# Sixteen pairs of heads transposed by transfers inside SBUF, their tokens loaded 96 apart

## The chip, the cores and the metric

The kernel runs on one core of a Trainium2 chip. The core has five engines that run side by side: TensorE (PE, matmuls and transposes), VectorE (DVE), ScalarE (ACT), GpSimd (POOL) and SyncE (SP, which here only issues transfers), and 16 DMA engines that carry them out. The metric is the time of one execution on the device in microseconds (us), lower is better. Three runs of the kernel before took 293.79, 295.81 and 297.07 us; their median is 295.81 us.

## The reference

An attention layer with a few "beacon" keys in front, then a feed-forward layer whose three inner products go through a maximum:

```
B, H, S, Nb, D = 8, 8, 576, 16, 64
k_all, v_all = concat(beacon_k, k), concat(beacon_v, v)      # 592 keys
scores = q @ k_all.T / sqrt(D)        # causal on the 576, beacons always seen
attn   = softmax(scores) @ v_all
x = attn as (4608 tokens, 512)
h = max(x @ w1, x @ w2, x @ w3)       # 512 -> 768
out = h @ w_out                       # 768 -> 512, fp32
```

## The kernel before

**Units.** Two heads of one batch are a pair; there are 4 pairs per batch and 32 in all (p = 4 * batch + place). For the scores a pair needs q and k with the 64 features of both heads on the 128 partitions and the tokens along the free dimension. This transposed form lies in the tile `qkT`, which has `NT` = 4 slots (pair p uses slot p % 4), each with a q part and a k part of 16 beacon columns and 576 tokens.

**Three ways into `qkT`.** The first four pairs have a way of their own. Twenty of the other pairs (4 to 15, and the even ones from 16 on) go by `load_cast`: POOL issues two transfers that read fp32 from DRAM and write bf16 to a tile `p16`; one burst before the pair is needed, `turn_cast` makes 24 transposes on PE into PSUM, and two copies (the q part by ACT, the k part by DVE) bring them to `qkT`. The eight odd pairs from 17 on (the list `BY_DMA`) go by transfers: `load_pair` has SP load q and k as fp32 into a tile `st`, `cast_pair` casts them to bf16 on POOL, `store_pair` writes that to a scratch tensor `qk_dram` in DRAM, and `fetch_pair` brings it back with one transposing transfer. In both ways partition j of the loaded tile holds the six consecutive tokens 6j to 6j+5 of a head, which is one run of 1536 bytes in DRAM.

**The loop.** From batch 1 on, the causal part of the scores of a batch is cut into 13 windows of 512 columns, and three windows make a burst; there are 31 bursts, c = 0 to 30, and a pair's scores take a little over one. `loop` writes the order of the work out by hand, burst by burst, each engine and queue in that order: the score matmuls of the burst's windows (`emit_window`, with the exponential on ACT), two units of the feed-forward layer, the beacon columns and the PE transposes of pairs that the next burst needs, the masks on POOL, the products with v for pairs whose scores were done in the burst before (`emit_pv`), the stores of finished output rows, what stands in `late` (`store_pair` four bursts and `fetch_pair` two bursts ahead of the pair's first burst), then the casts on POOL that are due (`jobs`), and feed-forward units up to a fixed count of about 5.08 per burst. A block of 512 tokens is 18 units of the first product and 4 of the second, so about one block per batch.

**Loads.** `jobs` also sets the loads: the loads for SP (v in two pieces per batch, and the pairs of `BY_DMA`) stand in one list; four are issued at the start, and each cast then issues the next one. A load lands in one of 5 `st` buffers, so that it waits for the cast five loads before it.

**The attention output.** From batch 2 on, when the last pair of a batch is through, SP issues five transposing transfers (`fetch_x`, one per 128 tokens, from the tile `x` in SBUF to `xT` in SBUF) in that burst, behind the loads of the same burst. A feed-forward block waits for those of them that hold its tokens.

**SP's order.** Everything that SP issues (output rows, loads, stores to scratch, fetches of pairs and of x) leaves in program order; an entry that waits holds back those behind it.

The lines that the texts below name: 146 `load_pair`, 182 `cast_pair`, 194 `load_cast`, 220 `load_v`, 278 `store_pair`, 284 `fetch_pair`, 326 and 332 `turn_cast` (transposes, copies), 414 scores, 443 masks, 467 products with v, 505 `fetch_x`, 530 and 544 first product, 560 second product, 591 output stores.

Of the kernel before, what the change touches and what calls it, by code (L numbers as in the profile page):

```python
# [9 lines left out]
BF16 = mybir.dt.bfloat16  # L10
# [6 lines left out]
def kernel(  # L17
# [13 lines left out]
    nc = tc.nc  # L31

    B, H, S, D = q.shape
    Nb = beacon_k.shape[2]
    NK = S + Nb
# [7 lines left out]
    PPB = H // 2  # L43
    NPAIR = B * PPB
# [13 lines left out]
    QR = 6  # L58
    QP = S // QR
# [3 lines left out]
    part_p = [(hi - lo) // HR for lo, hi in part_tok]  # L63


    BY_DMA = [p for p in range(4 * PPB, NPAIR) if p % 2]
    X_PE = [0, 1]

    const = ctx.enter_context(tc.tile_pool(name="const", bufs=1))
# [1 line left out]
    pair_pool = ctx.enter_context(tc.tile_pool(name="pair", bufs=6))  # L71
# [2 lines left out]
    ffn_h = ctx.enter_context(tc.tile_pool(name="ffn_h", bufs=2))  # L74
    ffn_y = ctx.enter_context(tc.tile_pool(name="ffn_y", bufs=6))
    psum = ctx.enter_context(tc.tile_pool(name="psum", bufs=1, space=PSUM))
    dram_pool = ctx.enter_context(
        tc.tile_pool(name="dram", bufs=len(BY_DMA), space=bass.MemoryType.DRAM)
    )

    w_in = [const.tile([128, n_ct, d_ff], BF16, name=f"w{i}_sb") for i in range(3)]
    w_out_sb = const.tile([128, n_ft, d_model], BF16, name="w_out_sb")
# [18 lines left out]
    ident = const.tile([128, 128], BF16, name="ident")  # L101
# [3 lines left out]
    NT = 4  # L105
    qkT = const.tile([128, NT, 2, NKP], BF16, name="qkT")
# [31 lines left out]
    def load_pair(p, gate=None):  # L138
        b, pi = divmod(p, PPB)
        hs = slice(2 * pi, 2 * pi + 2)  # L140
        st = new_stage(("pair", p))
        if gate:
            gate.memset(st[0:QP, 0:1], 0.0)
            gate.memset(st[0:QP, NQ2 : NQ2 + 1], 0.0)
        for i, src in enumerate((q, k)):
            nc.sync.dma_start(
                out=st[0:QP, i * NQ2 : (i + 1) * NQ2].rearrange("p (h x) -> p h x", h=2),
                in_=src[b, hs].rearrange("h (p r) d -> p h (r d)", r=QR),
            )

    def part_source(i, h0, n, part):
# [26 lines left out]

    def cast_pair(p, cast):
        st = stage.pop(("pair", p))  # L180
        t16 = pair_pool.tile([QP, QR, 4, D], BF16, name="p16")
        cast(
            t16.rearrange("p r x d -> p x r d"),
            st[0:QP].rearrange("p (x r d) -> p x r d", x=4, r=QR),
        )
        stage["pair16", p] = t16

    def load_cast(p):
        b, pi = divmod(p, PPB)
        hs = slice(2 * pi, 2 * pi + 2)  # L190
        t16 = pair_pool.tile([QP, QR, 4, D], BF16, name="p16")
        t16 = t16.rearrange("p r x d -> p (r x d)").rearrange("p (x r d) -> p x r d", x=4, r=QR)
        for i, src in enumerate((q, k)):
            nc.gpsimd.dma_start(  # L194
                out=t16[:, 2 * i : 2 * i + 2].rearrange("p h r d -> p h (r d)"),
                in_=src[b, hs].rearrange("h (p r) d -> p h (r d)", r=QR),
            )
        stage["cast", p] = t16
# [72 lines left out]

    qk_dram = {}

    def store_pair(p):
        qk_dram[p] = dram_pool.tile([S, 4 * D], BF16, name="qk_dram")
        nc.sync.dma_start(
            out=qk_dram[p].rearrange("(p r) x -> p (r x)", r=QR),
            in_=stage.pop(("pair16", p)).rearrange("p r x d -> p (r x d)"),  # L280
        )

    def fetch_pair(p):
        nc.sync.dma_start_transpose(out=qkT[:, p % NT, :, Nb:NK], in_=qk_dram.pop(p))

    def turn_part(p, part, q_copy, k_copy):
        lo, hi = part_tok[part]
        n = part_p[part]
        for i in range(2):
            src = stage.pop(("part16", p, part, i))  # L290
            pb = one_bank().bitcast(BF16)[:, 0 : hi - lo]
            for r in range(HR):
                for e in range(2):
                    nc.tensor.transpose(
                        pb[64 * e : 64 * e + 64, r * n : (r + 1) * n],
                        src[:, e, r],
                        ident[0:n, 0:n],
                        tile_position=(0, 64 * e),
                    )
            dst = qkT[:, p % NT, i, Nb + lo : Nb + hi]  # L300
            (q_copy, k_copy)[i](
                dst.rearrange("d (p r) -> d p r", r=HR), pb.rearrange("d (r p) -> d p r", r=HR)
            )

    def turn_pair(p, q_copy, k_copy):
        src = stage.pop(("pair16", p))
        for i in (1, 0):
            pb = one_bank().bitcast(BF16)[:, 0:S]
            for r in range(QR):
                nc.tensor.transpose(  # L310
                    pb[:, r * QP : (r + 1) * QP],
                    src[:, r, 2 * i : 2 * i + 2].rearrange("p h d -> p (h d)"),
                    ident[0:QP, 0:QP],
                )
            (q_copy, k_copy)[i](
                qkT[:, p % NT, i, Nb:NK].rearrange("d (p r) -> d p r", r=QR),
                pb.rearrange("d (r p) -> d p r", r=QR),
            )

    def turn_cast(p, q_copy, k_copy):  # L320
# [310 lines left out]
    def L(fn, *a):  # L631
        return lambda: fn(*a)
# [167 lines left out]
    for b in range(2, B):  # L800
        c = first_burst[PPB * b]
# [18 lines left out]
    def X(b):  # L820
        avail[0] = S * (b + 1)
# [3 lines left out]
    def loop():  # L825
        nb = len(bursts)
        turns_x = []
        late = {}
        for p in range(PPB + 1, NPAIR):
            c = first_burst[p]  # L830
            if p in BY_DMA:
                late.setdefault(c - 4, []).append(L(store_pair, p))
                late.setdefault(c - 2, []).append(L(fetch_pair, p))
        for c, burst in enumerate(bursts):
            for w in burst:
                if w != ahead:
# [114 lines left out]
```

## Time and profile before

| | |
|---|---|
| profiled execution, own time | 294.89 us |
| its span on the core | 293.2 us |
| granted PE clock, mean | 0.994 |
| median of three runs without profile | 295.81 us |
| PE busy | 280.0 us, 95% of the span |
| DVE, ACT, POOL busy | 203.0, 123.5, 125.6 us |
| DMA moved | 43.37 MB in 89174 packets |

The span runs from the first to the last instruction of the program; the profiled execution's own time is 1.7 us longer. Busy time says how much an engine did, and the chain that ended last says what the end waited for. A transfer has two durations: how long the issuing queue was held (the duration of the issue), and how long until the data had landed. DMA packets are the pieces into which a transfer is cut; most of this kernel's are 256 bytes.

### The profile page before, as it was taken

The numbers are of one execution on the slowest core, as the hardware profiler recorded it, in microseconds if no ns is written. First come the engines' busy times: TensorE is split into PE (matmuls) and PEld (weight loads), VectorE is DVE, ScalarE is ACT, GpSimd is POOL, SyncE is SP. The second block draws the span as 40 slices with busy tenths as digits, with TensorE's granted clock in tenths as the row PEclk, the third lists the DMA queues.
The fourth block names the chain that finished last, engine by engine and source line by source line (L and its number), as shares of the span: only waits on it lengthen the run. The fifth ranks groups of instructions, "written<-read, shape, count | busy, mean of one in ns | idle before, by whom it ended". The sixth has DMA issues, their size and how long they took to land.

```text
span 293.2 us, 8074 instructions
## 1 busy us (share of the span) xinstructions
PE 280.0 (95%) x3146; PEld 161.4 (55%) x3146; DVE 203.0 (69%) x408; ACT 123.5 (42%) x270; POOL 125.6 (43%) x256
## 2 busy tenths in 40 slices
PE   7798897799999999999999999999999999999995
PEld 4566674366555555545555688755545554444442
DVE  4675877276877767766777677767756886785873
ACT  4655456469555445464554545445464300000000
POOL 8629534977836264736483544355321300000000
PEclk9999999799999999999999999999999999999999
DMA  8999999999974489769999995766183005103003
GB/s 152 198 205 124 168 197 201 220 221 294 226 164 57 100 230 238 145 123 201 245 238 194 234 226 99 122 189 118 25 106 139 0 18 155 54 2 123 20 1 143
DMA packets 89174, 43.37 MB, mean 148 GB/s; under 512 B 68400, under 2 KB 83888, under 8 KB 89136
## 3 DMA queue, kind: packets, MB, share of 16 engines
q1 hardware_dynamic: 73968, 32.63, 49.4%
q0 software_dynamic: 14816, 9.98, 24.6%
q8 instruction: 24, 0.39, 0.6%
q10 hardware_dynamic: 352, 0.25, 0.3%
q14 instruction: 14, 0.11, 0.1%
HBM read 35.13 MB, written 11.80 MB: 160 GB/s over the span
## 4 chain that ended last, share of the span: by engine, by line
PE 84%; DMA 10%; POOL 3%; DVE 1%; issue 1%; SPq 0%; POOLq 0%; DVEq 0%
PE ps L530 44%; PE ps L560 16%; PE ps L467 10%; DMA st<-in_v_dram 8%; PE ps L414 8%; PE ps L326 3%; DMA quad<-in_k_dram 2%; POOL v L233 1%; PE ps L544 1%; POOL quad L173 1%; PE ps L493 1%; POOL at L443 1%; PE ps L579 0%; DVE at L441 0%; POOL p L194 0%
## 5 line engine op out<-in xcount | busy, mean ns | idle before, releaser
L423 ACT ACTIVATE at<-ps 128x512 bf16<-128x512 f32 (+3 forms) x214 | 106.8, 598 | 102.2 <-PE ps L414 74.2
L530 PE MATMUL ps<-xT,w_sb 128*128 128x512 bf16 (+2 forms) x720 | 148.6, 354 | 0.1
L530 PEld LDWEIGHTS <-w_sb 128*128 128x128 bf16 x720 | 65.6, 98 | 57.7 <-issue 5.8
L443 POOL TENSOR_SCALAR_AFFINE_SELECT at<-at 128x256 bf16<-128x256 bf16 (+2 forms) x153 | 55.8, 386 | 94.8 <-ACT at L423 82.8
L522 DVE TENSOR_TENSOR hT<-hT,ps 128x512 bf16<-128x512 bf16 (+2 forms) x111 | 74.5, 673 | 30.7 <-PE ps L530 29.0
L520 DVE CAST hT<-ps 128x512 bf16<-128x512 f32 (+2 forms) x57 | 37.6, 662 | 15.9 <-PE ps L530 14.0
L560 PE MATMUL ps<-w_out_sb,hT 128*128 128x512 bf16 x210 | 48.5, 379 | 0.0
L467 PE MATMUL ps<-v,at 128*128 128x65 bf16 (+1 forms) x960 | 40.9, 194 | 4.5 <-POOL v L233 4.3
L467 PEld LDWEIGHTS <-at 128*128 128x128 bf16 (+1 forms) x960 | 36.4, 98 | 13.8 <-issue 5.0
L568 DVE COPY y<-ps 128x512 f32<-128x512 f32 x35 | 24.2, 692 | 25.5 <-PE ps L560 24.2
L414 PE MATMUL ps<-qkT 64*128 64x80 bf16 (+20 forms) x560 | 33.2, 253 | 1.6 <-DVE qkT L332 1.2
L479 DVE TENSOR_TENSOR x<-ps,recip 128x384 bf16<-128x384 f32 (+1 forms) x68 | 32.1, 472 | 2.4
L560 PEld LDWEIGHTS <-hT 128*128 128x128 bf16 x210 | 19.5, 98 | 23.2 <-DVE hT L522 1.2
L414 PEld LDWEIGHTS <-qkT 64*128 64x128 bf16 x560 | 18.7, 97 | 16.8 <-issue 11.3
L233 POOL CAST v<-st 128x512 bf16<-128x512 f32 (+2 forms) x33 | 22.4, 707 | 12.2 <-DMA st<-in_v_dram 12.1
L586 ACT COPY y<-ps 128x320 f32<-128x320 f32 x1 | 0.4, 426 | 56.4 <-PE ps L579 56.4
L332 DVE COPY qkT<-ps 128x576 bf16<-128x576 bf16 x24 | 17.7, 750 | 0.2
L477 DVE RECIPROCAL recip<-ps 128x6 f32<-128x6 f32 (+1 forms) x68 | 12.3, 181 | 4.9 <-PE ps L467 4.5
L326 PEld LDWEIGHTS <-p 96*64 96x64 bf16 x480 | 11.3, 110 | 7.5 <-issue 7.5
L326 PE MATMUL ps<-ident,p 96*64 96x96 bf16 x480 | 14.0, 208 | 0.0
L194 POOL DMA_DIRECT2D p<-in_q_dram x20 | 12.9, 644 | 0.9
L194 POOL DMA_DIRECT2D p<-in_k_dram x20 | 12.8, 638 | 0.0
(47 smaller groups left out, 96.2 us busy)
## 6 DMA issues: line engine op xcount, KB each, us to landing
out_dram<-y SPq DMA_DIRECT2D x35, 256.0 KB, 2.2
st<-in_v_dram SPq DMA_DIRECT2D x24, 256.0 KB, 6.8
p<-in_q_dram POOLq DMA_DIRECT2D x20, 144.0 KB, 5.2
p<-in_k_dram POOLq DMA_DIRECT2D x20, 144.0 KB, 5.8
st<-in_q_dram SPq DMA_DIRECT2D x8, 288.0 KB, 5.6
st<-in_k_dram SPq DMA_DIRECT2D x8, 288.0 KB, 5.6
qk_dram<-p SPq DMA_DIRECT2D x8, 288.0 KB, 4.3
st<-in_v_dram SPq DMA_DIRECT2D x8, 224.0 KB, 6.0
```

Of the source, the lines that this page charges most:

```text
L194: nc.gpsimd.dma_start(out=t16[:, 2 * i : 2 * i + 2].rearrange("p h r d -> p h (r d)"), in_=src[b, hs].rearrange("h (p r) d -> p h (r d)", ...
L233: cast(v_sbs[b % 2][0:n, t0:t, :, 0:D], st[0:n, (t0 - lo) * H * D : (t - lo) * H * D].rearrange("p (t h d) -> p t h d", h=H, d=D),)
L326: nc.tensor.transpose(pb[64 * e : 64 * e + 64, r * QP : (r + 1) * QP], src[:, 2 * i + e, r], ident[0:QP, 0:QP], tile_position=(0, 64 * e),)
L414: nc.tensor.matmul(banks[e][:, col : col + qb - qa], qkT[hs, s, 1, 128 * t : 128 * t + 128], qkT[hs, s, 0, Nb + qa : Nb + qb], start=True, ...
L423: nc.scalar.activation(out=at[:, e, base : base + width], in_=banks[e][:, 0:width], func=AF.Exp, scale=scale,)
L443: nc.gpsimd.affine_select(out=view, in_=view, compare_op=ALU.is_ge, fill=0.0, base=x0, pattern=[[0, 2], [1, w]], channel_multiplier=-1,)
L467: nc.tensor.matmul(bank[:, c : c + GW], at[0 : k_rows[t], e, a : a + 128], v_sb[0 : k_rows[t], t, 2 * pi + e, 0:GW], start=(t == 0), stop= ...
L479: nc.vector.tensor_mul(x.rearrange("p i (e d) -> p i e d", e=2), pv[:, :, :, 0:D], recip.to_broadcast([128, n, 2, D]),)
L520: (by_act if act else by_dve)(h, bank)
L522: nc.vector.tensor_max(h, h, bank)
L530: nc.tensor.matmul(bank[:, o0 : o0 + n], w_in[i][:, ct, 128 * ft : 128 * (ft + 1)], xT[:, ct, x0 : x0 + n], start=(ct == 0), stop=(ct == n ...
L560: nc.tensor.matmul(bank, hT[:, ft, 128 * tt : 128 * (tt + 1)], w_out_sb[:, ft, :], start=(ft == 0), stop=(ft == n_ft - 1),)
```

## The change

All sixteen pairs from 16 on go by transfers. The scratch in DRAM and `store_pair` are gone: `fetch_pair` transposes straight from the bf16 tile in SBUF to `qkT` in SBUF, as two transfers, k first, each turning 96 partitions of 6 x 128 values. For that, partition j of the loaded tile holds the tokens j, j+96, ..., j+480, so that a load consists of runs of one token (256 bytes of fp32), 1152 per transfer. `cast_pair` casts q and k in two instructions and puts the two heads of a token side by side. The loads, casts and fetches keep the due times that they had for the odd pairs. `turn_cast` is left to the pairs 4 to 15. `turn_pair` and the argument `gate` of `load_pair` weren't used.

```
-    BY_DMA = [p for p in range(4 * PPB, NPAIR) if p % 2]
+    BY_DMA = [p for p in range(4 * PPB, NPAIR)]
...
     def load_pair(p):
...
             nc.sync.dma_start(
-                out=st[0:QP, i * NQ2 : (i + 1) * NQ2].rearrange("p (h x) -> p h x", h=2),
-                in_=src[b, hs].rearrange("h (p r) d -> p h (r d)", r=QR),
+                out=st[0:QP, i * NQ2 : (i + 1) * NQ2].rearrange("p (x d) -> p x d", d=D),
+                in_=src[b, hs].rearrange("h (r p) d -> p (h r) d", p=QP),
             )
...
     def cast_pair(p, cast):
         st = stage.pop(("pair", p))
-        t16 = pair_pool.tile([QP, QR, 4, D], BF16, name="p16")
-        cast(
-            t16.rearrange("p r x d -> p x r d"),
-            st[0:QP].rearrange("p (x r d) -> p x r d", x=4, r=QR),
-        )
+        t16 = pair_pool.tile([QP, 2, QR, 2, D], BF16, name="p16")
+        for i in (1, 0):
+            cast(
+                t16[:, i],
+                st[0:QP, i * NQ2 : (i + 1) * NQ2].rearrange("p (h r d) -> p r h d", h=2, r=QR),
+            )
...
-    def store_pair(p):
-        qk_dram[p] = dram_pool.tile([S, 4 * D], BF16, name="qk_dram")
-        nc.sync.dma_start(
-            out=qk_dram[p].rearrange("(p r) x -> p (r x)", r=QR),
-            in_=stage.pop(("pair16", p)).rearrange("p r x d -> p (r x d)"),
-        )
-
     def fetch_pair(p):
-        nc.sync.dma_start_transpose(out=qkT[:, p % NT, :, Nb:NK], in_=qk_dram.pop(p))
+        src = stage.pop(("pair16", p))
+        for i in (1, 0):
+            nc.sync.dma_start_transpose(
+                out=qkT[:, p % NT, i, Nb:NK].rearrange("d (r p) -> d r p", r=QR),
+                in_=src[:, i].rearrange("p r h d -> p (r h d)"),
+            )
...
             if p in BY_DMA:
-                late.setdefault(c - 4, []).append(L(store_pair, p))
                 late.setdefault(c - 2, []).append(L(fetch_pair, p))
```

More of the change, by code (lines that the diff above doesn't have):

```diff
@@ L76 @@
     psum = ctx.enter_context(tc.tile_pool(name="psum", bufs=1, space=PSUM))
-    dram_pool = ctx.enter_context(
-        tc.tile_pool(name="dram", bufs=len(BY_DMA), space=bass.MemoryType.DRAM)
-    )
     w_in = [const.tile([128, n_ct, d_ff], BF16, name=f"w{i}_sb") for i in range(3)]
@@ L136, in new_stage, with load_pair @@
         return stage[key]
-    def load_pair(p, gate=None):
+    def load_pair(p):
         b, pi = divmod(p, PPB)
@@ L141, in load_pair @@
         st = new_stage(("pair", p))
-        if gate:
-            gate.memset(st[0:QP, 0:1], 0.0)
-            gate.memset(st[0:QP, NQ2 : NQ2 + 1], 0.0)
         for i, src in enumerate((q, k)):
             nc.sync.dma_start(
-                out=st[0:QP, i * NQ2 : (i + 1) * NQ2].rearrange("p (h x) -> p h x", h=2),
-                in_=src[b, hs].rearrange("h (p r) d -> p h (r d)", r=QR),
+                out=st[0:QP, i * NQ2 : (i + 1) * NQ2].rearrange("p (x d) -> p x d", d=D),
+                in_=src[b, hs].rearrange("h (r p) d -> p (h r) d", p=QP),
             )
@@ L190, in load_cast @@
         hs = slice(2 * pi, 2 * pi + 2)
-        t16 = pair_pool.tile([QP, QR, 4, D], BF16, name="p16")
-        t16 = t16.rearrange("p r x d -> p (r x d)").rearrange("p (x r d) -> p x r d", x=4, r=QR)
+        t16 = pair_pool.tile([QP, 2, QR, 2, D], BF16, name="p16")
+        t16 = t16.rearrange("p i r h d -> p (i r h d)").rearrange(
+            "p (x r d) -> p x r d", x=4, r=QR
+        )
         for i, src in enumerate((q, k)):
@@ L270, in turn_beacons @@
             by_act(bT[:, :, Nb * b0 : Nb * b1], pb)
-    qk_dram = {}
-    def store_pair(p):
-        qk_dram[p] = dram_pool.tile([S, 4 * D], BF16, name="qk_dram")
-        nc.sync.dma_start(
-            out=qk_dram[p].rearrange("(p r) x -> p (r x)", r=QR),
-            in_=stage.pop(("pair16", p)).rearrange("p r x d -> p (r x d)"),
-        )
-    def fetch_pair(p):
-        nc.sync.dma_start_transpose(out=qkT[:, p % NT, :, Nb:NK], in_=qk_dram.pop(p))
+    def fetch_pair(p):
+        src = stage.pop(("pair16", p))
[3 more added lines that the diff above has]
+                in_=src[:, i].rearrange("p r h d -> p (r h d)"),
+            )
     def turn_part(p, part, q_copy, k_copy):
@@ L302, in turn_part @@
                 dst.rearrange("d (p r) -> d p r", r=HR), pb.rearrange("d (r p) -> d p r", r=HR)
[L303 to L317, printed above, removed]
             )
```

## The prediction

> **What bounds the kernel now.** I read the page first: the busy times, the DMA queues and the chain of work that ended last.
>
> ```profile
> PE 280.0 (95%) x3146; PEld 161.4 (55%) x3146; DVE 203.0 (69%) x408; ACT 123.5 (42%) x270; POOL 125.6 (43%) x256
> ...
> q1 hardware_dynamic: 73968, 32.63, 49.4%
> q0 software_dynamic: 14816, 9.98, 24.6%
> ...
> PE 84%; DMA 10%; POOL 3%; DVE 1%; issue 1%; SPq 0%; POOLq 0%; DVEq 0%
> PE ps L530 44%; PE ps L560 16%; PE ps L467 10%; DMA st<-in_v_dram 8%; PE ps L414 8%; PE ps L326 3%; DMA quad<-in_k_dram 2%; POOL v L233 1%; PE ps L544 1%; POOL quad L173 1%; PE ps L493 1%; POOL at L443 1%; PE ps L579 0%; DVE at L441 0%; POOL p L194 0%
> ```
>
> PE is 84% of the chain, and the transposes of line 326 are a part of it. The change touches only the middle of the run, so I read the chain there in order of time (start, us, what):
>
> ```profile
> 136.39 0.77 PE ps L414 x16
> 137.15 1.83 PE ps L530 x8
> 138.99 0.63 PE ps L326 x24
> 139.62 0.47 PE ps L467 x12
> ...
> 164.03 0.77 PE ps L414 x16
> 164.79 1.85 PE ps L530 x16
> ```
>
> One piece follows the other with no gap: PE sets the pace of a burst, and the 24 transposes of a pair cost it 0.63 us. The scores at 136.39 open burst 16, those at 164.03 burst 20. What must not come late is what these pieces read: pair 19 has its first scores in burst 16, and the line 530 piece at 164.79 begins token block 4, which needs the first three `fetch_x` of batch 4.
>
> **The gain.** The group of these transposes on PE from 101.8 to 231.7 us:
>
> ```profile
> L326 PE MATMUL ps<-ident,p 96*64 96x96 bf16 x192 | 5.6, 208 | 0.0
> ```
>
> 192 are eight pairs of 24: the even pairs 16 to 30, all of which the change takes off PE. 8 x 0.63 = **5.04 us**, all on the chain. The two copies per pair on DVE and ACT go too; neither stands on the chain here, so I count nothing. At full gain the profiled execution of 294.89 us becomes 289.85.
>
> **POOL.** Its groups from 101.8 to 184 us, and the busy time of the engines in that stretch and the next (PE, PEld, DVE, ACT, POOL):
>
> ```profile
> L443 POOL TENSOR_SCALAR_AFFINE_SELECT at<-at 128x256 bf16<-128x256 bf16 (+2 forms) x55 | 20.1, 386 | 41.0 <-ACT at L423 35.7 <-ACT qkT L339 4.1 <-DMA out_dram<-y 0.6
> L182 POOL CAST p<-st 96x1536 bf16<-96x1536 f32 x6 | 8.9, 1477 | 0.0
> ...
> L194 POOL DMA_DIRECT2D p<-in_q_dram x6 | 3.9, 642 | 0.4
> L194 POOL DMA_DIRECT2D p<-in_k_dram x6 | 3.8, 637 | 0.0
> ```
> ```profile
> 101.80:184.00 82.20, 82.20 (x977) 49.46 (x978) 58.50 (x111) 40.70 (x89) 44.17 (x85) 1.00 0.96 197
> ```
>
> An even pair loses two issues (0.64 + 0.64 = 1.28 us) and gets a cast; every cast becomes two of half the size. The trace doesn't have a 96x768 cast: between 0.74 us (half of 1.48) and 1.48, so 1.5 to 3.0 per pair; I take 1.7, near the row, as the elements stay the same. That adds 0.4 us per even pair and 0.2 per odd one, 16 x 0.3 = 5 us on an engine with 38 of 82 us free. What hides it is the wait of the masks for ACT (35.7 us). If that cover were gone, the masks would come late and with them `emit_pv`, one burst later. The casts now wait for loads on SP; a load is issued four casts ahead, and with six loads per batch (two of v, four pairs) in 4.3 bursts of 6.9 us that is about 20 us.
>
> **SP's queue.** Here the price lies. Its timeline between the `fetch_x` of batch 3 and of batch 4, the first and last rows and the costly ones (start, us, what):
>
> ```profile
> 123.83 7.47 SPq L505 DMA_TRANSPOSE xT<-x  x5
> 131.41 1.24 SPq L284 DMA_TRANSPOSE qkT<-qk_dram  x1
> ...
> 133.37 3.24 SPq L591 DMA_DIRECT2D out_dram<-y  x4
> 136.71 1.08 SPq L146 DMA_DIRECT2D st<-in_q_dram  x1
> 137.84 0.82 SPq L146 DMA_DIRECT2D st<-in_k_dram  x1
> ...
> 141.65 7.10 SPq L220 DMA_DIRECT2D st<-in_v_dram  x5
> ...
> 152.62 0.57 SPq L278 DMA_DIRECT2D qk_dram<-p  x1
> 154.27 6.42 SPq L505 DMA_TRANSPOSE xT<-x  x5
> ```
>
> The fourteen rows before 154.27 add up to 27.2 us, so SP is already held for 27.2 of 30.4 us. The issue times by line (min/median/max in ns), with the times to landing of the two transposing transfers:
>
> ```profile
> L505 SPq DMA_TRANSPOSE xT<-x x30: 1185/1254/2543, 92.0 to 245.0; - x30
> ...
> DMA to landing us min/median/max: 2.3/2.7/5.2
> ```
> ```profile
> L284 SPq DMA_TRANSPOSE qkT<-qk_dram x8: 1244/1506/2177, 107.6 to 217.2; - x8
> ...
> DMA to landing us min/median/max: 3.2/5.9/7.2
> ```
> ```profile
> L220 SPq DMA_DIRECT2D st<-in_v_dram x40: 384/858/5652, 2.7 to 174.9; - x40
> ```
>
> In the new order SP issues between the same two points: five of `fetch_x`, five fetches of pairs (19 to 23) as ten transposing transfers, eight loads of q and k (pairs 25 to 28), eight of v (batches 5 and 6), four output rows. The three stores to scratch and three fetches from DRAM go. I let the stretch begin at the same 123.8: SP waits ahead of that point for a buffer that a cast of burst 13 frees, and that cast loses POOL's two issues (1.28 us) ahead of it, while SP gets two more v transfers behind it.
>
> - Ten transposing transfers SBUF to SBUF of 96x768. The nearest row is `fetch_x`, also SBUF to SBUF: 1.25 us for 512 columns, with 80, 112 or 128 partitions alike. The fetch from DRAM, 576x256, has the same floor (1.24). From below 1.2; from above, if it goes by blocks of 128 columns (six for four), 1.88. I take 1.25 and a gap of 0.05: 13.0 us.
> - Eight loads, now of 1152 runs of 256 bytes. The nearest row is a v load (1024 such runs): 0.38 when the queue is free, 7.10/5 = 1.42 when one follows the other. They come in twos and fours; I take 1.0: 8.0 us. Eight v transfers, one of them the small beacon one, more spread: 0.65, 5.2 us.
> - Output rows 4 x 0.4 = 1.6 (half of the 3.24 that the four take here, where they wait behind other transfers), `fetch_x` 6.5.
>
> Sum **34.3 us**; bounds 13.0 + 8 x 0.38 + 8 x 0.38 + 1.4 + 6.4 = 27 and 18.8 + 8 x 1.42 + 8 x 1.42 + 3.2 + 7.5 = 52.
>
> What is allowed: 30.4 us less what PE gains by then (pairs 16, 18, 20, 22: 2.5 us), plus the slack of the x of batch 4. Its third transfer starts at 154.27 + 2 x 1.25 = 156.8 and lands 2.7 (median) to 5.2 later, 159.5 to 162.0; read at 164.79, the slack is some 4.1 us. 30.4 - 2.5 + 4.1 = 32.0. So the x of batch 4 comes **2.3 us late** and PE waits at block 4. Earlier, pair 19: its k and q follow the `fetch_x` of batch 3, which ends near 131.3; the second transfer starts at 132.6, lands by the row of `fetch_x` at 135.3, and is wanted at 136.39 - 1.3 = 135.1: 0.2 us. Pairs after 24 have lighter bursts. Total waits **2.5 us**.
>
> **The DMA engines** have the same order of load. Packets and rates from 101.8 to 184, from 124 to 126 (v loads and `fetch_x`), from 171.5 to 176 (v loads):
>
> ```profile
> DMA packets 33202, 16.18 MB, mean 197 GB/s; under 512 B 27136, under 2 KB 31077, under 8 KB 33189
> ```
> ```profile
> DMA packets 1910, 0.48 MB, mean 240 GB/s; under 512 B 1910, under 2 KB 1910, under 8 KB 1910
> ```
> ```profile
> DMA packets 3365, 0.95 MB, mean 212 GB/s; under 512 B 3330, under 2 KB 3330, under 8 KB 3364
> ```
>
> In the stretch the new order moves 10 x 0.147 (transposes) + 8 x 0.295 (loads) + 1.64 (800 rows of v) + 0.59 (x) + 1.05 (output) = 7.1 MB. At 240 GB/s that takes 29.6 us, at 212 GB/s 33.5, against the same 32.0: no wait, or 1.5 us, much the same as SP's count and not on top of it. For the larger pieces that the change takes away, a stretch with loads in runs of 1536 bytes:
>
> ```profile
> 69.50:73.60 4.10, 4.10 (x84) 2.82 (x85) 2.79 (x8) 3.94 (x11) 3.12 (x8) 1.00 1.16 297
> ```
>
> [...] By the rate of the large pieces the stretch would take 7.1 / 0.297 = 24 us and never bind; by the small ones it is at the edge.
>
> **Sum.** 294.89 - 5.04 + 2.5 = 292.35 us for the profiled execution. The median of the runs shown is 0.92 above that execution; carried over it is 293.3. I say **292.5**.
>
> **Rivals.**
>
> *The queue eats the gain.* Same mechanism, worse rates: loads at 1.2 and v at 0.9 add 1.6 + 2.0 = 3.6 us of SP in the stretch. Time 292.35 + 3.6 = 296; with half of it 294. For it: 27.2 of 30.4 us held already. Against it: the scratch writes and the loads by POOL's queue leave the same engines.
>
> *Slower: the issue of a transposing transfer grows with its columns.* Then each holds SP for 1.88 us, the ten of the stretch cost 6.3 us more, and the fourteen others between 101.8 and 184 up to 4 us where PE catches up in between. 292.35 + 6.3 = 298.7 to 302.5. It decides from 1.25 + 2.5/10 = 1.5 us per issue on, where the whole gain is gone. For it: there is no row with six blocks. Against: rows with 80 and 128 partitions and one from DRAM all give 1.2 to 1.3. [...]
>
> *POOL waits for a load.* A landing beyond the 20 us of lead holds the masks; at 1 us in each of five bursts the gain is gone: 295. Against: the loads land within 9 us now.
>
> *It does not do what it says*, if the transposes ran in time that PE would wait anyway: 294.9. Against: the chain without gaps.
>
> **How the numbers follow.** Waits of 0 to 4 us, the forecast: 0.50, of which 0.36 by more than 1%, which is about what a measurement of this kernel can tell from no change (the three runs spread by 1.1%). The eaten gain 0.20 (0.02 still faster, 0.14 within 1%, 0.04 slower), the long issue 0.22, POOL 0.05 (0.03 slower), no effect 0.03. Faster 0.38, within 1% 0.33, slower 0.29. The likeliest case alone reaches from 289.9 to 294; the range goes to full gain less a little scatter, 289.5, and into the long issue, 301.
>
> **What would show it.** Right: line 326 falls from 480 to 288 transposes, the chain has no such piece after 101.8, `qk_dram` is gone, line 274 of the new file has 32 issues at about 1.25 us, PE waits of 1 to 3 us on `xT` near block 4, SP with hardly a wait between 105 and 185. Wrong: issues of 1.5 us and more, scores waiting for transfers to `qkT` in several bursts, casts waiting for loads, or no waits at all.

## The result, and the profile after

The changed kernel takes 305.45 us (median of four runs, 304.75 to 306.35), the kernel before 296.15 in the same comparison: a ratio of **1.033** with a 95% interval of 1.026 to 1.040, so 3.3% slower. The forecast of 292.5 missed, and on the wrong side. The profiled execution took 304.98 us with a span of 302.9, against 294.89 and 293.2 before. Where the 9.7 us of span come from can be read in three steps. Ratios, here and below, leave out executions that fell into a slower state, which stand in the medians of e3 (six of ten), e6 (two of four) and e10 (one of five), and the traces of e3 and e10 are of such executions (296.84 and 296.16 us). (Lines of the new file: 140 `load_pair`, 177 `cast_pair`, 212 and 217 `load_v`, 274 `fetch_pair`, 304 `turn_cast`, 392 scores, 445 products with v, 483 `fetch_x`, 508 first product, 538 second product, 569 output.)

The page first: busy times, the granted clock in 40 slices, the DMA queues, and the chain that ended last.

```profile
PE 278.3 (92%) x2954; PEld 159.8 (53%) x2954; DVE 197.6 (65%) x400; ACT 119.3 (39%) x262; POOL 128.5 (42%) x264
...
PEclk9999999799999999997999989999999999999999
...
DMA packets 128980, 45.71 MB, mean 151 GB/s; under 512 B 115120, under 2 KB 124464, under 8 KB 128944
...
q1 hardware_dynamic: 117104, 37.36, 61.8%
q0 software_dynamic: 11488, 7.62, 17.8%
...
PE 76%; DMA 11%; SPq 3%; POOL 3%; DVE 2%; ACT 2%; issue 1%; POOLq 0%; DVEq 0%; ACTq 0%
PE ps L508 44%; PE ps L538 12%; PE ps L445 9%; PE ps L392 8%; DMA xT<-x 4%; DMA st<-in_v_dram 3%; DMA qkT<-p 2%; DMA quad<-in_k_dram 2%; PE ps L304 2%; ACT at L401 2%; SPq L483 2%; SPq L274 1%; PE ps L522 1%; POOL v L230 1%; POOL quad L167 1%
```

The packets rose from 89174 to 128980, all of it on the hardware queue (SP's), which got 43000 more, and PE's share of the chain fell from 84% to 76%. New in the chain are `xT<-x`, `qkT<-p` and SP's own sequencer at lines 483 and 274: the middle of the run now waits for transposing transfers and for the queue that issues them.

Second, the list of what PE waited for (us in total, times, longest). The kernel before had neither of these two rows:

```profile
PE ps L508 <- DMA xT<-x: 7.0, 3, 4.0
...
PE ps L392 <- DMA qkT<-p: 3.8, 3, 2.4
```

Together 10.8 us, all between 133 and 206 us. Third, the busy times from 105 to 200 us (length, then PE, PEld, DVE, ACT, POOL; granted clock, DMA share, GB/s), first after and then before:

```profile
105.00:200.00 95.00, 86.04 (x889) 51.69 (x887) 57.96 (x113) 38.56 (x86) 48.03 (x95) 0.96 1.00 186
```
```profile
105.00:200.00 95.00, 95.00 (x1121) 57.44 (x1120) 67.17 (x129) 45.75 (x101) 50.38 (x97) 1.00 0.93 189
```

PE was never idle there before, and is now idle for 9.0 of 95 us; its mean clock is 0.96 in place of 1.00, which is some 3.4 us (two slow pieces, shown in the section on why the prediction was wrong). The loss shows in the busy time of the whole run too: 280.0 less the 5.6 of the transposes would be 274.4, and 278.3 is 3.9 more. PE's idle time rose from 293.2 - 280.0 = 13.2 to 302.9 - 278.3 = 24.6 us, which is 11.4: the 10.8 above and 0.6 more for v through POOL. The account of the span is then -5.6 (transposes) + 11.4 (idle) + 3.9 (slower matmuls, most of it the clock) = +9.7, as the spans say.

Why the transfers are late stands in SP's timeline (start, us, what), here from the fetch of pair 18 to the x of batch 4:

```profile
117.99 4.31 SPq L274 DMA_TRANSPOSE qkT<-p  x2
...
123.66 1.47 SPq L212 DMA_DIRECT2D st<-in_beacon_v_dram  x1
125.18 2.43 SPq L217 DMA_DIRECT2D st<-in_v_dram  x3
127.72 7.86 SPq L483 DMA_TRANSPOSE xT<-x  x5
135.67 2.53 SPq L274 DMA_TRANSPOSE qkT<-p  x2
138.30 0.53 SPq L140 DMA_DIRECT2D st<-in_q_dram  x1
...
163.03 3.97 SPq L274 DMA_TRANSPOSE qkT<-p  x2
167.09 1.15 SPq L217 DMA_DIRECT2D st<-in_v_dram  x2
168.34 6.41 SPq L483 DMA_TRANSPOSE xT<-x  x5
```

SP has one issue after the other from 107 to 176 us, with no pause above 0.3 us. The x of batch 3 starts at 127.72 and not at 123.83, and from there to the x of batch 4 it takes 40.6 us where it took 30.4. PE waits for both, and in between for pair 19 (with the wait before each piece in brackets):

```profile
135.04 1.89 PE L508 MATMUL ps<-xT,w_sb 128*128 128x512 bf16 x8 [1.23 <-DMA xT<-x]
...
139.56 1.15 PE L392 MATMUL ps<-qkT 64*128 64x128 bf16 x10 [2.36 <-DMA qkT<-p]
...
173.41 2.54 PE L508 MATMUL ps<-xT,w_sb 128*128 128x256 bf16 x12 [3.98 <-DMA xT<-x]
```

### The profile page after: what moved, and what is told of

Same layout as the page of the kernel before. It is cut to its first block, busy times and chain, and to the rows that moved or that the text cites. A ratio compares the mean times of both kernels' runs of the same rounds, so it can differ in the third digit from the quotient of the medians.

```text
span 302.9 us, 7738 instructions
## 1 busy us (share of the span) xinstructions
PE 278.3 (92%) x2954; PEld 159.8 (53%) x2954; DVE 197.6 (65%) x400; ACT 119.3 (39%) x262; POOL 128.5 (42%) x264
## 2 busy tenths in 40 slices
DMA packets 128980, 45.71 MB, mean 151 GB/s; under 512 B 115120, under 2 KB 124464, under 8 KB 128944
## 4 chain that ended last, share of the span: by engine, by line
PE 76%; DMA 11%; SPq 3%; POOL 3%; DVE 2%; ACT 2%; issue 1%; POOLq 0%; DVEq 0%; ACTq 0%
PE ps L508 44%; PE ps L538 12%; PE ps L445 9%; PE ps L392 8%; DMA xT<-x 4%; DMA st<-in_v_dram 3%; DMA qkT<-p 2%; DMA quad<-in_k_dram 2%; PE ps L304 2%; ACT at L401 2%; SPq L483 2%; SPq L274 1%; PE ps L522 1%; POOL v L230 1%; POOL quad L167 1%
## 5 line engine op out<-in xcount | busy, mean ns | idle before, releaser
L508 PE MATMUL ps<-xT,w_sb 128*128 128x512 bf16 (+2 forms) x720 | 150.2, 357 | 7.1 <-DMA xT<-x 7.0
L508 PEld LDWEIGHTS <-w_sb 128*128 128x128 bf16 x720 | 66.6, 99 | 66.5 <-issue 11.0
L445 PEld LDWEIGHTS <-at 128*128 128x128 bf16 (+1 forms) x960 | 37.5, 98 | 15.2 <-issue 5.7
L392 PE MATMUL ps<-qkT 64*128 64x80 bf16 (+20 forms) x560 | 34.5, 256 | 5.4 <-DMA qkT<-p 3.8
L392 PEld LDWEIGHTS <-qkT 64*128 64x128 bf16 x560 | 19.4, 98 | 21.1 <-issue 15.7
L177 POOL CAST p<-st 96x768 bf16<-96x768 f32 x32 | 25.5, 824 | 0.0
L310 DVE COPY qkT<-ps 128x576 bf16<-128x576 bf16 x16 | 11.7, 749 | 0.0
L304 PEld LDWEIGHTS <-p 96*64 96x64 bf16 x288 | 6.8, 110 | 4.5 <-issue 4.5
L294 DVE COPY qkT<-ps 128x336 bf16<-128x336 bf16 (+1 forms) x15 | 6.3, 456 | 3.7 <-PE ps L287 3.7
L304 PE MATMUL ps<-ident,p 96*64 96x96 bf16 x288 | 8.4, 208 | 0.0
```

Source lines behind the costliest of these rows:

```text
L177: cast(t16[:, i], st[0:QP, i * NQ2 : (i + 1) * NQ2].rearrange("p (h r d) -> p r h d", h=2, r=QR),)
L392: nc.tensor.matmul(banks[e][:, col : col + qb - qa], qkT[hs, s, 1, 128 * t : 128 * t + 128], qkT[hs, s, 0, Nb + qa : Nb + qb], start=True, ...
L445: nc.tensor.matmul(bank[:, c : c + GW], at[0 : k_rows[t], e, a : a + 128], v_sb[0 : k_rows[t], t, 2 * pi + e, 0:GW], start=(t == 0), stop= ...
L508: nc.tensor.matmul(bank[:, o0 : o0 + n], w_in[i][:, ct, 128 * ft : 128 * (ft + 1)], xT[:, ct, x0 : x0 + n], start=(ct == 0), stop=(ct == n ...
```

## The experiments

The theory after the result: one in-order queue is overrun, by the time that SP spends on each issue and by the DMA engines' backlog of small packets, which was taken to hold an issue longer (an assumption that no row shows). The rivals: the price of an issue grows with its size; one of these two burdens alone is to blame; the order in the queue is to blame. All edits are made to the changed kernel, and all ratios are to the kernel before.

**e1: the loads of pairs 17 to 31 issued by POOL.**

```
-            nc.sync.dma_start(
+            (nc.gpsimd if p > 16 else nc.sync).dma_start(
                 out=st[0:QP, i * NQ2 : (i + 1) * NQ2]...
```

> The changed kernel with the loads of the pairs 17 to 31 issued from POOL's queue instead of SP's; the same transfers, the same 256-byte packets. Theory A (the time for which SP's queue is held by issues is the bound): between the fetch_x of batch 3 and of batch 4 SP was held 40.6 us; it loses eight loads of some 1.1 us there and six more ahead of the first of these points, so that the x of batch 3 and 4 and pair 19 come in time: no PE waits on xT and qkT, 290 to 294 us. Theory B (the DMA engines are the bound, by twice as many packets under 512 bytes): the packets are the same, PE waits as before, 303 to 307 us. If POOL pays by the run (1152 for 192), POOL becomes late with the masks instead: 297 to 305 with waits on POOL.

306.18 us, ratio 1.034 (1.028 to 1.041): no gain at all. The queue lost the q and k loads (8.9 us in the stretch), and yet the x of batch 4 starts at 166.37, only 2 us earlier than in the changed kernel. SP's and PE's waits, and rows of SP's timeline:

```profile
SPq L212 <- POOL p L177: 7.7, 2, 6.4
```
```profile
PE ps L508 <- DMA xT<-x: 8.8, 2, 4.5
```
```profile
126.83 9.33 SPq L483 DMA_TRANSPOSE xT<-x  x5
...
151.68 6.02 SPq L217 DMA_DIRECT2D st<-in_v_dram  x3
157.79 5.18 SPq L274 DMA_TRANSPOSE qkT<-p  x2
```

The time came back in two ways. The loads of v had to wait 6.4 us for an `st` buffer that a cast on POOL frees, from 118.1 to 124.7, with the x of batch 3 in line behind them; that cast ended at 124.66, 3.2 us later than in the changed kernel, behind four load issues of 0.88 us each that POOL now makes. And the remaining issues got longer: five of x 9.33 us (7.86), three of v 6.02 (1.69), two transposing transfers up to 5.18 (3.97). Taking issues off SP alone didn't help. As e1 brings a wait of its own, it doesn't show that SP's issues cost nothing. Nor were the packets the same, as had been expected. From 105 to 200 us they are a third fewer than the 60550 of the changed kernel, because POOL's queue carries its loads as 2038 packets of some 3 KB, and nothing was gained:

```profile
DMA packets 40220, 18.48 MB, mean 195 GB/s; under 512 B 36980, under 2 KB 36980, under 8 KB 40209
q0 software_dynamic: 2038, 6.23, 33.1%
```

**e2: loads in runs of 1536 bytes.** This kernel reads the tokens in another order, so that pairs from 16 on compute scores of other tokens; every amount of work and of bytes stays.

```
-  .rearrange("p (x d) -> p x d", d=D), in_=src[b, hs].rearrange("h (r p) d -> p (h r) d", p=QP)
+  .rearrange("p (h x) -> p h x", h=2), in_=src[b, hs].rearrange("h (p r) d -> p h (r d)", r=QR)
```

> The changed kernel with the loads in runs of 1536 bytes as before the change (192 packets per load instead of 1152). The tokens come in another order, so that the scores are those of other tokens; everything else is left as it is. Theory A (SP's issue time): the number of issues on SP is the same, only the loads that were held behind others get shorter, 299 to 304 us. Theory B (the engines): some 19 thousand of the 60 thousand packets between 105 and 200 us go, 290 to 294 us.

297.85 us, ratio 1.008 (1.005 to 1.011), between the two ranges that were expected. The packets from 105 to 200 us, first of the changed kernel and then of e2:

```profile
DMA packets 60550, 17.70 MB, mean 186 GB/s; under 512 B 59130, under 2 KB 59130, under 8 KB 60538
```
```profile
DMA packets 43966, 18.79 MB, mean 198 GB/s; under 512 B 38352, under 2 KB 42545, under 8 KB 43953
```

With as many issues as in the changed kernel, but a quarter fewer packets, three quarters of the loss are gone. The stretch between the two fetches of x falls from 40.6 to 35.5 us: the eight loads from 8.9 to 5.0, the ten transposing transfers from 15.4 to 13.5. The price of an issue in a free queue explains little of the loads' 3.9 us: a load of k held SP for 0.58 us at the least with the short runs and 0.43 with the long ones, a load of q for 0.31 with both. So most of it is time for which a load was held behind others, and that the engines' backlog holds it is the reading that fits, not one that a row shows. PE still waits:

```profile
PE ps L392 <- DMA qkT<-p: 2.5, 3, 1.5
PE ps L508 <- DMA xT<-x: 1.9, 2, 1.7
```

**e3: one transposing transfer per pair.** q and k lie side by side in the bf16 tile and in `qkT`; the one transfer turns 96 x 1536.

```
-        for i in (1, 0):
-            nc.sync.dma_start_transpose(
-                out=qkT[:, p % NT, i, Nb:NK].rearrange("d (r p) -> d r p", r=QR),
-                in_=src[:, i].rearrange("p r h d -> p (r h d)"),
-            )
+        nc.sync.dma_start_transpose(
+            out=qkT[:, p % NT, Nb : Nb + 2 * S].rearrange("d (r p) -> d r p", p=QP),
+            in_=src.rearrange("p i r h d -> p (i r h d)"),
+        )
```

> The changed kernel with k and q of a slot of qkT side by side, so that one transposing transfer of 96 x 1536 takes the place of two of 96 x 768: 16 issues for 32, the same packets. If an issue costs 1.26 us whatever its columns: theory A gives 290 to 294 us (SP loses five issues of 1.5 us in the stretch and three ahead of it), theory B 303 to 307. If the issue of twelve blocks costs twice that of six, both give 303 to 306.

296.31 us, ratio 0.993 (0.989 to 0.998). Here the packets stay and the issues of pairs are halved, and the kernel is 4% faster than the changed one by the ratios (3% by the medians, which put it level with the kernel before); both expected ranges were missed. The issue times by line (ns, min/median/max), first of the changed kernel with 96 x 768, then of e3 with 96 x 1536:

```profile
L274 SPq DMA_TRANSPOSE qkT<-p x32: 1206/1264/2652, 107.5 to 228.0; - x32
```
```profile
L273 SPq DMA_TRANSPOSE qkT<-p x16: 1295/1689/2792, 107.6 to 218.6; - x16
```

Twice the columns cost 1.30 us at the least against 1.21: at its floor an issue has nearly one price for both sizes. The median is 1.69 against 1.26, still well under twice; how much of that is the size and how much the full queue isn't parted. The rival of the long issue is out: the changed kernel's own median of 1.264 us is a third below the 1.88 that it needs.

**e4: the new path for the odd pairs alone** (`if p % 2` is back in `BY_DMA`; the even pairs go by PE again).

> The changed kernel with only the odd pairs from 17 on by transfers, as before the change, and the even ones by PE: the path inside SBUF and the 256-byte runs alone, without the eight further pairs. Theory A: SP issues two transposing transfers (2.6 us) for a store and a fetch (2.2 us), and loads some 0.5 us longer per pair: no more held than before, 294 to 297 us. Theory B: 15 thousand packets more than before instead of 40 thousand, 296 to 300 us.

296.73 us, ratio 1.001 (0.998 to 1.005). For the odd pairs, trading the scratch for two transfers in SBUF costs and brings nothing that can be measured. The stretch is 33.0 us and PE waits 0.7 for `qkT`. All of the loss comes with the even pairs.

**e5: x ahead of the loads.** `fetch_x` moves in front of the loads of its burst.

```
+            for p in pvs:
+                b, pi = divmod(p, PPB)
+                if b not in X_PE and pi == PPB - 1:
+                    for i in range(n_qt):
+                        fetch_x(b, i)
+                    at_burst(c + 1, L(X, b))
             while jobs and jobs[0][0] <= c:
```

> The changed kernel with the five fetch_x of a batch issued ahead of the loads of the same burst, not behind them. If what is lost is lost by the place in SP's order (four v transfers and two loads stand ahead of the x of batch 3), the waits on xT (7.0 us on PE) go and 297 to 300 us remain. If it is lost by the sum that SP and the engines have to get through, the waits only move to the fetches of pairs: 302 to 306 us.

307.1 us, ratio 1.035 (1.031 to 1.038): no better than the changed kernel. The waits changed places, from x to the pair behind it:

```profile
PE ps L392 <- DMA qkT<-p: 8.2, 2, 5.5
...
PE ps L508 <- DMA xT<-x: 2.4, 1, 2.4
```

The x of batch 3 went out 2.1 us earlier (125.65), and pair 19, now behind the loads that x overtook (its transfers start at 138.03, in the changed kernel at 135.67), was waited for 5.5 us. In this queue the order only chose who was late.

**e6: e2 and e3 together** (again with scores of other tokens).

> The changed kernel with both relieved: loads in runs of 1536 bytes (tokens in another order, so the scores are of other tokens) and one transposing transfer per pair. If the engines' work on small packets and SP's issues are the whole loss, PE has no wait left and the time is 296.2 less 5.0: 290.5 to 292.5 us. If something else is lost as well (the casts on POOL, waits for buffers), it stays above 294.

293.5 us as median of four, ratio 0.981 (0.976 to 0.986) from two of them; 295.73 x 0.981 = 290.1. By the ratio that is about the full gain of 5.04 us, 1.7% of 294.89; by the median of all four it is less than half of it (0.992). The stretch is 33.6 us, the x of batch 3 starts at 122.38, and PE waits 1.7 us:

```profile
PE ps L391 <- DMA qkT<-p: 1.7, 2, 0.9
```

**e7: e3 with x ahead of the loads**, as in e5.

> One transposing transfer per pair and the fetch_x ahead of the loads, the rest as in the changed kernel. With one transfer alone PE still waited 2.4 us for xT and 1.6 to 2.4 us for qkT. If the order is worth something once the sum is smaller: 291.5 to 294 us. If not: 295 to 297, as with one transfer alone.

299.12 us, ratio 1.009 (1.004 to 1.013), slower than either range that was expected and worse than e3: 5.2 us of waits for `qkT`, 0.7 for x.

**e8: e7 with the even pairs on the new path from 24 on only** (`BY_DMA`: `p % 2 or p >= 6 * PPB`).

> As the run before it, but the even pairs 16 to 22 stay with PE; by transfers go the odd pairs from 17 on and all from 24 on. PE keeps four transposes of pairs (2.5 us) and loses four. The transfers of the dense bursts 11 to 18 fall by a third. If these bursts are where the waits come from: no wait on PE and 296.2 - 2.5 = 293.7, 292.5 to 294.5 us; if the waits follow the late pairs as well: 295 to 297.

294.59 us, ratio 0.996 (0.993 to 0.999). The bursts of the pairs 16 to 23 are where SP is overrun; with their even pairs on PE, most of e7's loss is gone, but one wait of 1.6 us stays.

**e9: e3 with the same `BY_DMA`,** x behind the loads as it was.

> One transposing transfer per pair, by transfers go the odd pairs from 17 on and all from 24 on, the fetch_x behind the loads as in the changed kernel. With the fetch_x ahead the same set took 294.59 (ratio 0.9958), PE waiting 1.6 us for qkT near 137 us. For all sixteen pairs the order behind the loads was the better one by 2.8 us; if that holds here, the wait goes: 292.5 to 294 us, faster than both kernels. If the order is worth nothing here: 294 to 295.

293.96 us, ratio 0.990 (0.988 to 0.993), and no wait of PE for `xT` or `qkT`. Four even pairs are moved, 4 x 0.63 = 2.5 us or 0.85%; the ratio gives 1.0%. Where the queue keeps up, the gain of the transposes arrives.

**e10 and e11: loads with the cast, by POOL's queue.** Each pair is read by four transfers that turn fp32 into bf16 on the way and land in the bf16 tile; SP's loads, the `st` buffer and POOL's casts of these pairs go, and one transfer turns the pair, as in e3. In e10 for the even pairs, in e11 for all sixteen.

```
+    def load_apart(p):
...
+        for i, src in enumerate((q, k)):
+            for h in range(2):
+                nc.gpsimd.dma_start(
+                    out=t16[:, 1 - i, :, h],
+                    in_=src[b, 2 * pi + h].rearrange("(r p) d -> p r d", p=QP),
+                )
...
-        if p in BY_DMA:
+        if p in BY_DMA and p % 2 == 0:        (e11: if p in BY_DMA:)
+            jobs.append((first_burst[p] - 5, None, L(load_apart, p)))
+        elif p in BY_DMA:
```

> All sixteen pairs by one transposing transfer each; the even ones are loaded and cast by POOL's queue (four transfers per pair, 96 apart, straight into the tile that is turned), so that SP issues neither their loads nor POOL casts them. Theory of a sum of two resources: SP loses 16 issues of 0.5 to 1 us, the engines' bytes read stay the same: 293 to 296 us, PE waits of 3 us or less. If what competes at the engines decides, as when all loads went by POOL: 297 to 303 us, with transposing transfers that land after 5 us and more.

> All sixteen pairs loaded and cast by POOL's queue, straight into the tile that is turned, and turned by one transposing transfer each; SP keeps v, output rows, x and 16 turns. Against the run before it (even pairs alone by POOL, ratio 0.9807, stretch between the x of batch 3 and 4 30.0 us) SP loses 16 more loads. If SP's sum still costs: 288 to 290.5 us. If it no longer does and the two queues only meet at the engines: 291 to 294, with transposing transfers that land later than 5 us in the median.

290.66 us, ratio 0.981 (0.977 to 0.984), and 290.5 us, ratio 0.980 (0.975 to 0.986): both beat the kernel before, by about the full gain (e10 lies below both of the ranges expected). The sixteen loads that e11 takes off SP beyond e10 bring nothing that can be measured. In e11 PE waits for neither `xT` nor `qkT`. POOL pays for it and has the room (same columns as above; the DMA share adds up the times of packets and comes to 1.41 here, so they overlap):

```profile
105.00:200.00 95.00, 94.25 (x1011) 57.08 (x1022) 66.25 (x130) 45.54 (x101) 70.77 (x135) 1.00 1.41 173
```

PE 94.25 of 95 us busy at full clock; POOL 70.8 against 48.0. e1 and e11 differ in two things, though: the kind of load, and one turn or two.

**e12: e11 with two transposing transfers per pair,** as in the changed kernel. It parts the two.

> All sixteen pairs loaded and cast by transfers of POOL's queue, straight into the bf16 tile, as in e11, but turned by two transposing transfers each, as in the changed kernel. It parts the two differences between e1 (loads by POOL as fp32, two turns, 1.034) and e11 (loads with the cast by POOL, one turn, 0.980). SP issues ten transposing transfers between the x of batch 3 and of batch 4 and no loads of q and k: 15.1 + 4.5 (v) + 2.3 (output) + 7.9 (x) = 29.8 us at the lengths of the changed kernel, under the 30.4 of the kernel before. Theory 1 (SP's issues and the engines' backlog both hold one queue; either relieved far enough is enough): close to the full gain, 290 to 293 us, ratio 0.98 to 0.99, PE waits on transposed tiles under 2 us. Theory 2 (two transposing transfers per pair are the trouble whatever else stands in the queue): the x of batch 4 is late, 297 to 302 us, waits of 4 us and more.

290.3 us, ratio **0.982** (0.976 to 0.988), the full gain with 32 issues of transposing transfers. Its packets from 105 to 200 us are nearly all below 512 bytes, and PE waits for no transposed tile:

```profile
DMA packets 68099, 16.35 MB, mean 172 GB/s; under 512 B 66245, under 2 KB 66245, under 8 KB 68085
```

SP's rows:

```profile
118.34 1.99 SPq L228 DMA_DIRECT2D st<-in_v_dram  x2
120.44 8.09 SPq L494 DMA_TRANSPOSE xT<-x  x5
...
144.51 4.61 SPq L285 DMA_TRANSPOSE qkT<-p  x2
149.21 1.15 SPq L228 DMA_DIRECT2D st<-in_v_dram  x2
150.53 3.37 SPq L285 DMA_TRANSPOSE qkT<-p  x2
153.99 7.15 SPq L494 DMA_TRANSPOSE xT<-x  x5
```

The issues are no shorter than in the changed kernel (a row of two takes up to 4.61 us), and from 107 to 175 us SP makes no pause above 0.6 us, not even for a buffer of `st`. But the x of batch 3 starts 7.3 us earlier and the stretch is 33.6 us. So two turns per pair are not the trouble by themselves, nor are small packets, nor a queue without pauses: what counts is whether what the queue holds is through when it is due.

The kernels side by side. The stretch runs from the first `fetch_x` of batch 3 to that of batch 4; the waits are PE's for `xT` and `qkT`; the clock is PE's from 105 to 200 us:

| kernel | ratio | x of batch 3 starts | stretch, us | PE waits, us | clock |
|---|---|---|---|---|---|
| before | 1 | 123.83 | 30.4 | 0 | 1.00 |
| changed | 1.033 | 127.72 | 40.6 | 10.8 | 0.96 |
| e1 loads by POOL, fp32 | 1.034 | 126.83 | 39.5 | 11.1 | 0.95 |
| e5 x first | 1.035 | 125.65 | 43.6 | 10.6 | 0.93 |
| e7 one turn, x first | 1.009 | 122.39 | 39.1 | 5.9 | 0.98 |
| e2 long runs | 1.008 | 125.21 | 35.5 | 4.4 | 1.00 |
| e4 odd pairs only | 1.001 | 125.40 | 33.0 | 0.7 | 1.00 |
| e8 e7, even pairs late | 0.996 | 120.50 | 36.4 | 1.6 | 1.00 |
| e3 one turn | 0.993 | 126.31 | 37.2 | 4.0 | 1.00 |
| e9 e3, even pairs late | 0.990 | 126.11 | 32.5 | 0 | 1.00 |
| e6 long runs, one turn | 0.981 | 122.38 | 33.6 | 1.7 | 1.00 |
| e10 even pairs by POOL, one turn | 0.981 | 125.63 | 30.0 | 3.0 | 0.98 |
| e12 all by POOL, two turns | 0.982 | 120.44 | 33.6 | 0 | 1.00 |
| e11 all by POOL, one turn | 0.980 | 120.52 | 32.2 | 0 | 1.00 |

With all the even pairs moved, stretches of 30 to 34 us go with the full gain, and those of the three slowest kernels are 39.5 us and more. In between the length alone doesn't order the kernels (e2 and e3): the fetches of pairs have due times of their own.

## Why the prediction was wrong

**The gain: right.** 480 transposes became 288, and PE's chain has no piece of line 304 in the middle. Where nothing is late (e11, e12), the ratio shows 1.8 to 2.0% against the 1.7% of 5.04 us; in e9 half the pairs give half of it.

**POOL: right.** The new cast took 0.824 us, two per pair 1.65 against the 1.7 taken. POOL's busy time rose by 2.9 us over the run; 5 were counted. PE's wait for v through POOL is 4.9 us, and was 4.3 before.

```profile
L177 POOL CAST p<-st 96x768 bf16<-96x768 f32 x32 | 25.5, 824 | 0.0
```

**The issue of a transposing transfer: right in its floor.** The median is 1.264 us against 1.25, and the rival of 1.88 fell with e3. The 1.88 was an estimate, 6/4 of 1.25, for a price that goes with the columns. By it 12 column blocks would cost twice 6, which no run shows: at the least they cost 1.30 us against 1.21.

**SP's stretch: this is the step that failed, twice.**

*Its start.* "I let the stretch begin at the same 123.8" was wrong by 3.9 us. SP's order was summed up only from the `fetch_x` of batch 3 on. But pairs 16 and 18 are fetched ahead of it. SP's rows there, of before and of after:

```profile
107.57 1.96 SPq L284 DMA_TRANSPOSE qkT<-qk_dram  x1
...
116.05 0.45 SPq L146 DMA_DIRECT2D st<-in_k_dram  x1
122.73 1.01 SPq L220 DMA_DIRECT2D st<-in_v_dram  x2
```
```profile
107.48 2.76 SPq L274 DMA_TRANSPOSE qkT<-p  x2
...
111.58 2.52 SPq L274 DMA_TRANSPOSE qkT<-p  x2
```

Before, there was one fetch of 1.96 us, and SP stood idle from 116.5 to 122.7. Now it fetches pairs 16, 17 and 18 in 2.76 + 2.52 + 4.31 = 9.6 us; the slack was spent, and more, before the stretch began. The argument named one condition of the start, the buffer that a cast frees, and not the other, the queue ahead of it.

*Its sum.* 34.3 us were taken and 40.6 measured. By terms: ten transposing transfers 15.4 (13.0 taken), eight loads 8.9 (8.0), v 4.5 (5.2), output 2.4 (1.6), x 7.9 (6.5), gaps between the rows 1.6 (counted within the transfers alone). Most of the 6.3 us are in the transposing transfers, of pairs and of x (2.4 + 1.4), and in the gaps (1.6): the transfers were set at the median issue, and the gaps were left out for all but ten. A few long issues make up the excess, as the median of line 274 stayed at 1.264 us and its longest took 2.652. What lengthened them isn't shown; the kernel before has one of 2.543 in line 505 too. That leaves the x of batch 4 ready 10 us later than forecast: its third transfer was to land at 123.83 + 34.3 + 2.5 + 2.7 = 163.3 and PE got it at 173.4, which is 3.9 + 6.3.

**The DMA engines: "not on top of it" was wrong.** SP's count (34.3) and the engines' count (29.6 to 33.5) came out alike, and the larger was taken. The 40.6 measured lie above both and far below their sum of more than 60: the two ran neither fully side by side nor one after the other. Two neighbouring stretches of the changed kernel (same columns as above):

```profile
133.00:140.70 7.70, 4.12 (x45) 2.08 (x43) 2.64 (x6) 0.77 (x2) 0.71 (x1) 0.92 0.51 100
140.70:147.90 7.20, 7.20 (x64) 3.49 (x64) 4.54 (x9) 2.70 (x7) 4.87 (x9) 0.85 1.10 282
```

In the first SP issues transposing transfers and small pieces one by one and the engines move 100 GB/s, with half their time empty; in the second they run full at 282 GB/s on loads and output rows. So the half-empty stretch isn't made up for by the full one. e2 shortens the one part, e3 the other, and each gets back over 2%; together they get 5%. e2 with its longer runs loses less than the changed kernel (1.008 against 1.033), but e12 has the full gain with 66245 of its 68099 packets below 512 bytes and at 172 GB/s, so this kernel's full gain needs neither long runs nor a high rate. The 297 GB/s of the prediction are no clean row for runs of 1536 bytes: only 0.33 of the 1.22 MB moved in that window went by POOL's queue, which carried those loads.

**The waits counted once.** "Total waits 2.5 us" rested on one late transfer, and on "pairs after 24 have lighter bursts". There were six waits, the last at 204 us, of 10.8 us in sum. In this queue, which made no pause above 0.3 us from 107 to 176 us, each lateness was handed on to the next transfer.

**The clock was not in the sum.** PE ran at half its clock in two pieces (0.50 from 139.6 to 140.7 us and from 174.0 to 177.0), each behind waits and for some 3.4 us:

```profile
140.70:143.00 2.30, 2.30 (x7) 0.81 (x7) 0.44 (x1) 2.30 (x6) 1.38 (x4) 0.52 1.26 266
143.00:145.50 2.50, 2.50 (x39) 1.63 (x38) 2.04 (x5) 0.06 (x1) 2.39 (x4) 1.00 1.10 366
```
```profile
173.40:175.40 2.00, 1.99 (x11) 1.48 (x11) 0.69 (x1) 0.00 (x0) 0.00 (x0) 0.56 0.52 107
175.40:177.40 2.00, 2.00 (x22) 1.66 (x21) 1.34 (x3) 0.00 (x0) 0.00 (x0) 0.59 0.80 304
177.40:179.40 2.00, 2.00 (x34) 1.85 (x32) 1.43 (x5) 0.00 (x0) 0.00 (x0) 1.00 0.77 191
```

At half clock, means of 0.56 and 0.59 over 2.0 us each are 1.8 + 1.6 = 3.4 us of slow time from 173.6 on; the first piece began at 139.5, as the 0.92 of the stretch from 133 to 140.7 shows, and ended near 142.9. Each costs 1.7 us, together 3.4. A wait of 4 us thus cost nearer 6. The slow piece from 173.6 us follows the wait of 3.98 us; the one from 139.5 follows two waits of 1.23 and 2.36 us that are each shorter, with 2.2 us of work between them. In e10, where PE waited twice for `qkT`, 3.0 us in sum and 2.4 at the longest, the page's clock has a 7 (tenths) in the slice from 184 to 191 us. In e2 and e3, whose single waits for `xT` and `qkT` are 1.75 and 2.45 us at most, the mean from 105 to 200 us stays at 1.00. So the length of a wait alone doesn't decide in these runs, and what does isn't shown.

**The rivals.** *The queue eats the gain* named the mechanism and gave 296, with 2.5 + 3.6 = 6.1 us of waits. It was the right one by kind; 10.8 us of waits and 3.9 of slower matmuls came, because it too let the stretch start on time, let the engines' part vanish, and left out the clock. The range's upper end of 301 came from the long issue, which wasn't so, while the bound of this same stretch, 52 us, was written down and given no time: by it the end is 292.35 + 52 - 34.3 = 310, and the range would have held the result. *POOL waits for a load* and *no effect* are out by the rows above.

**The signs.** "Scores waiting for transfers to `qkT` in several bursts" was on the list for wrong, and came; "SP with hardly a wait between 105 and 185" was on the list for right, and came too. The second was read as health. In the changed kernel SP made no pause because its queue was behind; but e12's makes hardly any either and loses nothing, so this sign tells neither way. What tells is when a transfer starts against when it is due.

**What stays open.** e1 fails and e12 succeeds with loads on the same queue of POOL; they differ in the cast on the way, in the size of the packets, in the `st` buffers and in the casts on POOL. The 6.4 us for which SP waited in e1 are as long as the start of x lies apart (126.83 against 120.44), which points to the buffers; a kernel that takes away this wait alone wasn't tried. That the queue was late is shown by e3, e9 and e12, which relieve it in different ways; what makes single issues long, a backlog at the engines or something else, is argued and not shown.

## What to carry to other kernels

Count an in-order transfer queue as you count an engine: everything it issues, from the last point where it stood idle, with the gaps, and with issue times as they are in a full queue. The larger of issue time and engine time was too little here (34.3 for 40.6 us), their sum would have been far too much, and a bound that is written down gets a time and a chance. Slack in one stretch isn't there if the change fills the stretch ahead of it. Here the change pays (290.3 against 296 us) once the loads leave that queue, cast on the way and land where they are turned, without a staging buffer that the queue's other loads wait for; which of these three does it wasn't parted.

## What the runs showed of the hardware that was not expected

A transposing transfer held SP for 1.2 to 1.3 us at the least whether it turned 96 x 768 or 96 x 1536. Halving the number of transfers for the same bytes (e3 against the changed kernel) was worth 3 to 4%.

The engines can be slack while their queue is behind: 100 GB/s at a share of 0.51 from 133 to 140.7 us, with no pause of SP. A low DMA share doesn't clear a queue. Nor does a high one convict it: e11 and e12 have shares of 1.41 and 1.44 of the 16 engines' time from 105 to 200 us, at 173 and 172 GB/s, and are among the fastest.

The number of packets from 105 to 200 us doesn't order the kernels either: 40220 in e1 (ratio 1.034), 60550 in the changed kernel (1.033), 43966 in e2 (1.008), 68099 in e12 (0.982).
